# One transfer for a unit's q and k, one for its v, and most of the first bias loads on GpSimd's DMA queue

## The chip, the core and the metric

The kernel runs on one core of a Trainium2 chip. The metric is the device time of one execution in microseconds (us), here the median of three runs. One further execution was recorded by the hardware profiler; "the profile" and "the trace" are of that one. TensorE (PE) multiplies, VectorE (DVE) and ScalarE (ACT) do elementwise work, GpSimd (POOL) does some of it too, and SyncE (SP) issues DMA transfers.

## What is computed

Attention with a relative position bias, and a feed-forward layer behind it, cut to what matters:

```python
# q, k, v: (4, 8, 576, 64) f32;  w1 (1, 32), b1 (32), w2 (32, 8)
scores = q @ k.T / sqrt(64)
rel = log1p(abs(i - j)) / log1p(max(i, 1))           # 576 x 576
bias = relu(rel[..., None] @ w1 + b1) @ w2           # 576 x 576 x 8 heads
attn = softmax(scores + bias)                        # over the last axis
x = (attn @ v)   # 4 x 576 tokens by 8 heads x 64
out = leaky_relu(x @ w_in, 0.01) @ w_out             # (2304, 512) -> 2048 -> 512
```

The bias depends on the head and the two positions, not on the batch.

## The kernel before

The work has three stages. **Bias generation** makes the bias for all heads. Its 36 row groups of 16 rows each (the list `GEN`) go through four relu tiles (`gen_r`, on ACT at L120 and on DVE at L122, shared out by a plan that balances the two engines), matmuls (`gen_mm`, L133), two ACT copies out of PSUM (`gen_ev`, L140 and L141) and one write of 295.5 KB to DRAM (L152). These DRAM buffers are five chunks, "0", "1", "2", "3" of 128 rows and "M" of 64. **Attention** runs over 16 units; a unit is a pair of heads and one batch entry, and has nine tiles in the order A0, B0, A1, B1, M, A2, B2, A3, B3. A tile's scores are made on PE (L242, or L233 for M, in unit 0; L248 after that), DVE adds the bias and takes the extreme (L271), ACT takes the exponential (L279), PE transposes (L313, L317, L331), ACT copies out (L329), and a multiplication by v follows twice per unit (L350). **The feed-forward layer** comes last; its weights are converted during attention.

All row groups are issued before the first tile: `gen_tick(g)` is called for g = -1 to 38, and a tick makes the relu tiles of group g + 1, the matmuls of group g and the copies and the write of group g - 1. The bias tiles of the first pair of heads are read back from DRAM by `load_bias(0, c)`, called at given ticks: chunk 0 at tick 16, chunk 1 at 24, M at 27, chunks 2 and 3 at 37. Chunk 0 is complete with the write of tick 10, chunk 1 with that of tick 18, M with tick 20, chunk 2 with tick 28, chunk 3 with tick 36. A load of a numbered chunk is three transfers (L174 for the A tile, L175 and L176 for the B tile); M is two (L170, L171).

Every engine works through its own instructions in order, in the order of the calls in the source (a hand-written schedule). Every transfer but one is issued by SP, so a transfer that waits for data holds back the later ones. `load_unit` loads a unit's q and k with four transfers (L186): q into rows 0 to 63 and again into rows 64 to 127, then k in the same way. `load_v` loads v with one transfer (L192) and the last 64 keys with two small ones (L194) into a tile whose other half DVE sets to zero at the start (L68, L69). Units 0 and 1 are loaded before the bias generation, unit u + 2 during unit u.

GpSimd has hardly anything to do before 51 us: it makes an identity matrix, scales `w2` (L93), and then waits for the first subtraction of unit 1 (L213). It issues no transfer.

The lines that order all this at the start and at each tick:

```python
        gen_setup()
        for u in range(2):
            load_unit(u)
            load_v(u)
...
        for c in {16: "0", 24: "1", 27: "M", 37: "23"}.get(g, ()):
            load_bias(0, c)
```

Of the kernel before, what the change touches and what calls it, by code (L numbers as in the profile page):

```python
# [8 lines left out]
F32 = mybir.dt.float32  # L9
# [14 lines left out]
KW = 2 * S + 64  # L24
# [15 lines left out]


@with_exitstack
def attention_ffn(ctx: ExitStack, tc: tile.TileContext, qt, kt, vm, vt, wi, wo, cst, out):
    nc = tc.nc
    PS = bass.MemoryType.PSUM
    xp = ctx.enter_context(tc.tile_pool(name="xp", bufs=1))
# [12 lines left out]
    def pstile(tag):  # L59
        shape = [128, 1024] if tag == "s" else [128, 512]  # L60
        return ps.tile(shape, F32, tag=tag, name="ps_" + tag)

    raw_b = [[ap.tile([128, c], F32, name=f"raw{c}{i}") for c in (2 * S, KW)] for i in range(2)]
    ident = ap.tile([128, 128], F32, name="ident")
    make_identity(nc, ident[:])
    vt_b = [ap.tile([128, 2, 64], F32, name=f"vt{i}") for i in range(3)]
    for t in vt_b:
        nc.vector.memset(t[0:64, 1, :], 0.0)  # L68
        nc.vector.memset(t[64:128, 0, :], 0.0)  # L69
    qs_b = [ap.tile([128, 1024], F32R, name=f"qs{i}") for i in range(2)]  # L70

    PT = ap.tile([128, 2, 10, HS], F32, name="PT")

    raw_0 = [gp.tile([128, c], F32, name=f"raw{c}") for c in (2 * S, KW)]
    cs = gp.tile([128, S + 214], F32, name="cs")
    bps = gp.tile([128, 144], F32, name="bps")
    warm = gp.tile([128, 1], F32, name="warm")
# [23 lines left out]
    for T in GEN:  # L101
# [3 lines left out]
        eng = ""  # L105
# [6 lines left out]
    def gen_r(g):  # L112
        T = GEN[g]
        w = gen_w(T)
        r = gr[T] = [None] * 4
        for q, c in enumerate(plan[g]):
            k = 4 * T + q
            t = gp.tile([128, S], F32, tag="r", name="r", bufs=9)
            if c == "a":
                nc.scalar.activation(out=t[:, :w], in_=ltw[:, :w], func=AF.Relu, bias=bps[:, k:k + 1])  # L120
            else:
                nc.vector.tensor_scalar(out=t[:, :w], in0=ltw[:, :w], scalar1=bps[:, k:k + 1], scalar2=0.0, op0=ALU.add, op1=ALU.max)  # L122
            r[q] = t

    def gen_mm(T):
        r = gr.pop(T)
        w = gen_w(T)
        pt = pstile("s" if w > 512 else "to"[T % 2])
        cuts = [(0, w)] if w <= 512 else [(0, w // 2), (w // 2, w)]
        o0 = 512 - w // 2 if w > 512 else 0  # L130
        for a, b in cuts:
            for q in range(4):
                nc.tensor.matmul(pt[32 * q:32 * q + 32, o0 + a:o0 + b], w2d, r[q][:, a:b], start=True, stop=True)  # L133
        gps[T] = pt, o0

    def gen_ev(T):
        pt, o0 = gps.pop(T)
        R, F = 16 * T + 15, S - 16 * T
        e = e_b[GEN.index(T) % len(e_b)]
        nc.scalar.activation(out=e[:, R:W], in_=pt[:, o0:o0 + F], func=AF.Copy, scale=ips[:, T:T + 1])  # L140
        nc.scalar.activation(out=e[:, 0:R], in_=pt[:, o0 + R:o0:-1], func=AF.Copy, scale=ips[:, T:T + 1])  # L141
        if T < 16:
            c, r0 = str(T // 8), 16 * (T % 8)
        elif T < 18:
            c, r0 = "M", 16 * (T - 16)
        elif T < 34:
            c, r0 = str(2 + (T - 18) // 8), 16 * ((T - 18) % 8)
        else:
            c, r0 = "M", 32 + 16 * (T - 34)
        a = r0 * H * PIT + 1  # L150
        dst = scr[c][a:a + 16 * (H * PIT + 1)].rearrange("(i x) -> i x", i=16)[:, 0:H * PIT].rearrange("i (h p) -> i h p", h=H)[:, :, 0:W]
        nc.sync.dma_start(out=dst, in_=e)  # L152

    def gen_tick(g):
        if g + 1 < 36:
            gen_r(g + 1)
        if 0 <= g < 36:
            gen_mm(GEN[g])
        if 0 <= g - 1 < 36:
            gen_ev(GEN[g - 1])  # L160
        for c in {16: "0", 24: "1", 27: "M", 37: "23"}.get(g, ()):
            load_bias(0, c)
    bias = {}

    def load_bias(hp, c):
        n = 64 if c == "M" else 128
        rows = scr[c][0:n * H * PIT].rearrange("(i h p) -> i h p", h=H, p=PIT)[:, :, 16:16 + S]
        if c == "M":
            t = ap.tile([128, S], F32, tag="biasM", name="biasM", bufs=1)
            nc.sync.dma_start(out=t[0:64, :], in_=rows[:, 2 * hp, :])  # L170
            nc.sync.dma_start(out=t[64:128, :], in_=rows[:, 2 * hp + 1, :])  # L171
        else:
            t = ap.tile([128, 2, S], F32, tag="bias", name="bias", bufs=5)
            nc.sync.dma_start(out=t[:, 0, :], in_=rows[:, 2 * hp, :])  # L174
            nc.sync.dma_start(out=t[:, 1, 64:S], in_=rows[:, 2 * hp + 1, 0:512])  # L175
            nc.sync.dma_start(out=t[:, 1, 0:64], in_=rows[:, 2 * hp + 1, 512:S])  # L176
        bias[hp, c] = t

    raw, qk, vv = {}, {}, {}

    def load_unit(u):
        hp, b = divmod(u, B)
        q_, k_ = raw_b[u % 2] if u else raw_0
        for t, src in ((q_, qt), (k_, kt)):
            for p in (0, 64):
                nc.sync.dma_start(out=t[p:p + 64], in_=src[hp, b])  # L186
        raw[u] = (q_, k_)

    def load_v(u):
        hp, b = divmod(u, B)  # L190
        v_ = ap.tile([128, 4, 128], F32, tag="v", name="v", bufs=3)
        nc.sync.dma_start(out=v_[:], in_=vm[hp, b])  # L192
        for h in range(2):
            nc.sync.dma_start(out=vt_b[u % 3][64 * h:64 * h + 64, h, :], in_=vt[hp, b, h])  # L194
        vv[u] = v_

    def split_hi(u, what):
        q_, k_ = raw[u]
        if what == "q":
            qs = qs_b[u % 2]  # L200
            nc.vector.tensor_copy(qs[:].rearrange("p (a c) -> p a c", a=2), q_[:].rearrange("p (a c) -> p a c", a=2)[:, :, 64:S])  # L201
            ks1 = ap.tile([128, KW], F32R, tag="ks1", name="ks1", bufs=2)
            ks2 = ap.tile([128, KW], F32R, tag="ks2", name="ks2", bufs=2)
            qk[u] = (qs, ks1, ks2)
        else:
            nc.vector.tensor_copy(qk[u][1][:], k_[:])

    def split_lo(u, what, a):
        q_, k_ = raw[u]
# [128 lines left out]
    def pv():  # L338
        _, u, g = pv_q.pop(0)
        hp, b = divmod(u, B)  # L340
        o, pt = outs.pop((u, g)), PT[:, g]
        if (u, g) == (HP * B - 1, 1):
            o = pstile("s")
        for jb in range(5):
            for h in range(2):
                if jb < 4:
                    l, r = vv[u][:, jb, 64 * h:64 * h + 64], pt[:, 2 * jb + h, :]
                else:
                    l, r = vt_b[u % 3][:, h, :], pt[:, 8, :]
# [233 lines left out]
    with tc.manual_schedule():  # L583
# [249 lines left out]
```

## Time and profile before

| what | value |
|---|---|
| median of three runs | 684.1 us (684.05 to 684.8) |
| the profiled execution's own time | 684.88 us |
| its span, first to last instruction | 683.1 us |
| PE busy | 672.4 us, 98% of the span |
| DVE, ACT, POOL busy | 72%, 60%, 30% |
| moved by DMA | 117.85 MB, of them 116.96 on SP's queue |

The page of the profile cuts the span into 40 slices and gives the busy share of each engine in tenths. Timelines name a start, a duration, an engine, a line of the kernel, output and input tiles, a count where alike instructions stand together, and in brackets the time in which the engine stood idle before it and what ended that wait. A matmul's end is modelled, so that "busy" on PE covers some latency. DMA share is the mean busy share of the 16 DMA engines, including the time in which a packet waits.

### The profile page before, as it was taken

The numbers are of one execution on the slowest core, as the hardware profiler recorded it, in microseconds if no ns is written. First come the engines' busy times: TensorE is split into PE (matmuls) and PEld (weight loads), VectorE is DVE, ScalarE is ACT, GpSimd is POOL, SyncE is SP. The second block draws the span as 40 slices with busy tenths as digits, with TensorE's granted clock in tenths as the row PEclk, the third lists the DMA queues.
The fourth block names the chain that finished last, engine by engine and source line by source line (L and its number), as shares of the span: only waits on it lengthen the run. The fifth ranks groups of instructions, "written<-read, shape, count | busy, mean of one in ns | idle before, by whom it ended". The sixth has DMA issues, their size and how long they took to land.

```text
span 683.1 us, 11880 instructions
## 1 busy us (share of the span) xinstructions
PE 672.4 (98%) x4240; PEld 548.9 (80%) x4240; DVE 490.4 (72%) x1080; ACT 409.2 (60%) x886; POOL 205.8 (30%) x227
## 2 busy tenths in 40 slices
PE   7999999999999999999999999999999999999997
PEld 3436778887778777787889898888989898988986
DVE  7987789999999998589999868534343754343342
ACT  7997778888878888685555455333333543333332
POOL 0005445666666653420000503111114512111110
PEclk9999999999999999999999999999999999999999
DMA  8997679668955976135367336533323345332202
GB/s 226 350 315 198 198 224 245 170 203 276 272 165 164 315 217 197 57 114 199 94 201 244 141 95 230 196 113 108 107 108 108 121 175 197 140 109 108 107 1 92
DMA packets 39931, 117.85 MB, mean 173 GB/s; under 512 B 9024, under 2 KB 13760, under 8 KB 37440
## 3 DMA queue, kind: packets, MB, share of 16 engines
q1 hardware_dynamic: 39728, 116.96, 53.8%
q8 instruction: 33, 0.54, 0.3%
q14 instruction: 26, 0.21, 0.1%
q10 hardware_dynamic: 144, 0.13, 0.1%
HBM read 86.78 MB, written 30.29 MB: 171 GB/s over the span
## 4 chain that ended last, share of the span: by engine, by line
PE 92%; ACT 3%; DMA 3%; DVE 2%; issue 1%; SPq 0%; DVEq 0%; ACTq 0%
PE ps_t L516 24%; PE ps_s L557 19%; PE ps_o L350 12%; PE ps_s L248 10%; PE ps_o L557 10%; PE ps_t L313 9%; PE ps_s L233 1%; PE ps_o L302 1%; PE ps_o L331 1%; DMA w1a<-w 1%; ACT x L140 1%; ACT r L120 1%; PE ps_s L133 1%; PE ps_t L133 1%; PE ps_o L133 1%
## 5 line engine op out<-in xcount | busy, mean ns | idle before, releaser
L528 DVE TENSOR_TENSOR c<-ps_t,c 128x384 f32<-128x384 f32 x164 | 88.8, 554 | 130.5 <-PE ps_t L516 129.4
L535 ACT ACTIVATE g<-c 128x384 fp32r<-128x384 f32 x96 | 50.4, 525 | 180.8 <-DVE c L528 156.7
L557 PE MATMUL ps_s<-ws,g 128*128 128x512 f32 x576 | 148.3, 393 | 0.0
L557 PEld LDWEIGHTS ps_s<-ws,g 128*128 128x128 f32 x576 | 106.7, 188 | 16.9
L271 DVE CUSTOM_DVE_ANT_0 p<-ps_s,bias 128x576 f32<-128x576 f32 x128 | 95.4, 752 | 21.7 <-PE ps_s L248 18.0
L279 ACT ACTIVATE p<-p,mx 128x576 f32<-128x576 f32 x128 | 99.8, 780 | 7.8 <-DVE mx L271 5.5
L516 PE MATMUL ps_t<-xo,w1c 128*128 128x384 f32 x504 | 99.8, 336 | 0.7 <-DVE c L528 0.6
L466 POOL TENSOR_TENSOR ws<-y,ws 128x512 fp32r<-128x512 f32 x32 | 42.7, 1334 | 184.2 <-PE ps_t L516 147.4
L329 ACT COPY PT<-ps_t 128x512 f32<-128x512 f32 x128 | 73.8, 577 | 39.9 <-PE ps_t L313 39.9
L516 PEld LDWEIGHTS ps_t<-xo,w1c 128*128 128x128 f32 x504 | 89.3, 188 | 8.7 <-DVE c L528 2.3
L248 PE MATMUL ps_s<-ks,qs 128*128 128x288 f32 x480 | 93.7, 317 | 0.0
L516 PE MATMUL ps_t<-xo,w1a 128*128 128x384 f32 x474 | 93.2, 335 | 0.0
L516 PEld LDWEIGHTS ps_t<-xo,w1a 128*128 128x128 f32 x474 | 84.4, 188 | 5.9
L248 PEld LDWEIGHTS ps_s<-ks,qs 128*128 128x128 f32 x480 | 67.6, 189 | 13.3 <-issue 4.8
L313 PE MATMUL ps_t<-ident,p 128*128 128x128 f32 x512 | 77.5, 274 | 0.0
L557 PE MATMUL ps_o<-ws,g 128*128 128x512 f32 x288 | 74.1, 393 | 0.0
L540 DVE TENSOR_TENSOR g<-gf,g 128x384 fp32r<-128x384 f32 x96 | 61.1, 636 | 14.5 <-ACT gf L536 14.4
L313 PEld LDWEIGHTS ps_t<-ident,p 128*128 128x128 f32 x512 | 61.0, 140 | 9.1 <-issue 8.2
L350 PE MATMUL ps_o<-PT,v 128*64 128x288 f32 x496 | 67.0, 412 | 0.0
L213 POOL TENSOR_TENSOR qs<-raw,qs 64x512 fp32r<-64x512 f32 x30 | 37.8, 1279 | 75.4 <-DVE qs L201 72.0
L557 PEld LDWEIGHTS ps_o<-ws,g 128*128 128x128 f32 x288 | 53.4, 188 | 8.5
L350 PEld LDWEIGHTS ps_o<-PT,v 128*64 128x64 f32 x496 | 32.9, 136 | 23.6 <-issue 2.9
(127 smaller groups left out, 908.9 us busy)
## 6 DMA issues: line engine op xcount, KB each, us to landing
w1a<-w SPq DMA_DIRECT2D x10, 1792.0 KB, 7.4
w1c<-w SPq DMA_DIRECT2D x9, 1792.0 KB, 7.4
raw<-kt SPq DMA_DIRECT2D x32, 304.0 KB, 5.9
raw<-qt SPq DMA_DIRECT2D x32, 288.0 KB, 4.4
w<-w1a SPq DMA_DIRECT2D x20, 448.0 KB, 5.6
raw<-wi SPq DMA_DIRECT2D x16, 512.0 KB, 3.9
raw<-wo SPq DMA_DIRECT2D x16, 512.0 KB, 4.6
scr<-x SPq DMA_DIRECT2D x21, 295.5 KB, 5.0
```

The source lines that it names most:

```text
L248: nc.tensor.matmul(s_[:, S0 + HS * hh:S0 + HS * hh + HS], qs[:, c0:c0 + 128], ks[:, k0 + HS * hh:k0 + HS * hh + HS], start=(j == 0), stop= ...
L271: nc.vector.tensor_tensor_reduce(out=p, in0=s_[:, S0:S0 + S], in1=bt, scale=-0.125, scalar=3.4e38, op0=ALU.add, op1=ALU.min, accum_out=i)
L279: nc.scalar.activation(out=p, in_=p, func=AF.Exp, bias=i, scale=-1.0, accum_out=sm)
L313: nc.tensor.transpose(t0[:, 128 * jb:128 * jb + 128], p[:, p0 + 128 * jb:p0 + 128 * jb + 128], ident[:])
L329: nc.scalar.copy(out=PT[:, g, 0:8, c].rearrange("p (j h) c -> p j h c", h=2)[:, :, h, :], in_=t0[:].rearrange("p (j c) -> p j c", j=4))
L350: nc.tensor.matmul(o[64 * h:64 * h + 64, 0:HS], l, r, start=(jb == 0), stop=(jb == 4))
L466: eng.tensor_sub(t[:, 1], y2[c % MF][:], t[:, 0].bitcast(F32))
L516: nc.tensor.matmul(o, w[:, a, PROD[j], c], x[:, b, k, :], start=(n == 0), stop=(n == 5))
L528: nc.vector.tensor_add(a if c == src else c_new(g, c), bank[g, j], a)
L535: nc.scalar.activation(out=t[:, 0], in_=h, func=AF.Prelu, alpha=0.01)
L540: nc.vector.tensor_sub(t[:, 1], gf.pop((g, c))[:], t[:, 0].bitcast(F32))
L557: nc.tensor.matmul(o, t[:, a, c], w[:, b], start=(m == 0 and n == 0), stop=(m == NG - 1 and n == 5))
```

## The change

A unit's q and k come as one transfer of 128 rows from an input that the host has laid out that way (both copies of q and k stand in DRAM; 9472 bytes per row). v and its last 64 keys, zeros included, come as one transfer of five 128-column blocks; the small tiles, their two transfers and their zeroing go. `load_bias(0, c)` for c other than "3" is issued from GpSimd, and is called at other ticks: chunk 0 at 12 (was 16), 1 at 20 (24), M at 23 (27), 2 at 30 (37); chunk 3 stays on SP at 37. Loads for the later pairs of heads stay on SP. The matmul with the last 64 keys (L350) takes its weights from the fifth block.

```diff
-    raw_b = [[ap.tile([128, c], F32, name=f"raw{c}{i}") for c in (2 * S, KW)] for i in range(2)]
+    raw_b = [ap.tile([128, 2 * S + KW], F32, name=f"raw{i}") for i in range(2)]
...
-    vt_b = [ap.tile([128, 2, 64], F32, name=f"vt{i}") for i in range(3)]
-    for t in vt_b:
-        nc.vector.memset(t[0:64, 1, :], 0.0)
-        nc.vector.memset(t[64:128, 0, :], 0.0)
...
-        for c in {16: "0", 24: "1", 27: "M", 37: "23"}.get(g, ()):
+        for c in {12: "0", 20: "1", 23: "M", 30: "2", 37: "3"}.get(g, ()):
             load_bias(0, c)
...
     def load_bias(hp, c):
+        eng = nc.sync if hp or c == "3" else nc.gpsimd
...
-            nc.sync.dma_start(out=t[:, 0, :], in_=rows[:, 2 * hp, :])
-            nc.sync.dma_start(out=t[:, 1, 64:S], in_=rows[:, 2 * hp + 1, 0:512])
-            nc.sync.dma_start(out=t[:, 1, 0:64], in_=rows[:, 2 * hp + 1, 512:S])
+            eng.dma_start(out=t[:, 0, :], in_=rows[:, 2 * hp, :])
+            eng.dma_start(out=t[:, 1, 64:S], in_=rows[:, 2 * hp + 1, 0:512])
+            eng.dma_start(out=t[:, 1, 0:64], in_=rows[:, 2 * hp + 1, 512:S])
...
     def load_unit(u):
         hp, b = divmod(u, B)
-        q_, k_ = raw_b[u % 2] if u else raw_0
-        for t, src in ((q_, qt), (k_, kt)):
-            for p in (0, 64):
-                nc.sync.dma_start(out=t[p:p + 64], in_=src[hp, b])
-        raw[u] = (q_, k_)
+        t = raw_b[u % 2] if u else raw_0
+        nc.sync.dma_start(out=t[:], in_=qk_in[hp, b])
+        raw[u] = (t[:, 0:2 * S], t[:, 2 * S:2 * S + KW])

     def load_v(u):
         hp, b = divmod(u, B)
-        v_ = ap.tile([128, 4, 128], F32, tag="v", name="v", bufs=3)
-        nc.sync.dma_start(out=v_[:], in_=vm[hp, b])
-        for h in range(2):
-            nc.sync.dma_start(out=vt_b[u % 3][64 * h:64 * h + 64, h, :], in_=vt[hp, b, h])
+        v_ = ap.tile([128, 5, 128], F32, tag="v", name="v", bufs=3)
+        nc.sync.dma_start(out=v_[:], in_=v_in[hp, b])
         vv[u] = v_
...
-                if jb < 4:
-                    l, r = vv[u][:, jb, 64 * h:64 * h + 64], pt[:, 2 * jb + h, :]
-                else:
-                    l, r = vt_b[u % 3][:, h, :], pt[:, 8, :]
+                l, r = vv[u][:, jb, 64 * h:64 * h + 64], pt[:, 2 * jb + h if jb < 4 else 8, :]
```

## Rows read from the trace of the kernel before

**Rows 1.** The page's 40 slices of the span, TensorE
```profile
PE   7999999999999999999999999999999999999997
```

**Rows 2.** Windows: span, busy us (count) by engine, PE clock, DMA share, GB/s
```profile
6.00:8.00 2.00, 2.00 (x21) 1.24 (x17) 1.92 (x5) 1.26 (x4) 0.00 (x0) 1.00 0.99 224
16.00:18.00 2.00, 2.00 (x18) 0.87 (x14) 2.00 (x6) 2.00 (x6) 0.00 (x0) 1.00 1.08 402
```

**Rows 3.** The same windows, around the end of bias generation and unit 0
```profile
56.00:58.00 2.00, 1.50 (x11) 0.94 (x11) 1.46 (x6) 1.50 (x4) 1.09 (x4) 1.00 0.94 280
58.00:60.00 2.00, 2.00 (x16) 1.45 (x15) 1.88 (x6) 2.00 (x6) 2.00 (x2) 1.00 1.01 278
```

**Rows 4.** Timeline of VectorE and TensorE around unit 0's sixth and eighth tiles
```profile
53.42 1.11 DVE L206 CAST ks<-raw 128x1216 fp32r<-128x1216 f32 x1
...
55.70 0.76 DVE L271 CUSTOM_DVE_ANT_0 p<-ps_s,bias 128x576 f32<-128x576 f32 x1 [1.17 <-DMA bias<-scr]
55.74 0.27 PE L331 MATMUL ps_o<-ident,p 128*128 128x128 f32 x1
...
56.52 0.76 PE L242 MATMUL ps_s<-raw,raw 64*128 64x288 f32 x4 [0.50 <-DVE mx L271]
...
58.07 0.76 DVE L271 CUSTOM_DVE_ANT_0 p<-ps_s,bias 128x576 f32<-128x576 f32 x1 [0.58 <-DMA bias<-scr]
```

**Rows 5.** The chain that ended last: start, us, what
```profile
51.49 4.08 DMA bias<-scr
```

**Rows 6.** Timeline of SP's transfers: start, us to issue, count
```profile
1.63 1.24 SPq L186 DMA_DIRECT2D raw<-qt  x2
...
11.88 1.23 SPq L152 DMA_DIRECT2D scrM<-e  x2
...
26.82 0.55 SPq L174 DMA_DIRECT2D bias<-scr  x1
...
42.61 8.82 SPq L152 DMA_DIRECT2D scr<-x  x9
...
55.05 0.32 SPq L174 DMA_DIRECT2D bias<-scr  x1
```

**Rows 7.** Bias tiles until 65 us: issue ns least/median/most, landing
```profile
L174 SPq DMA_DIRECT2D bias<-scr x4: 320/574/813, 26.8 to 55.0; - x4
...
DMA to landing us min/median/max: 2.8/4.1/5.1
```

**Rows 8.** Timeline of VectorE: the start, the relu tiles of the generation, tile A0
```profile
3.51 0.30 DVE L90 TENSOR_SCALAR bps<-cs 128x144 f32<-128x144 f32 x1 [1.69 <-DMA cs<-cst]
3.72 0.65 DVE L92 TENSOR_SCALAR cs<-cs 128x320 f32<-128x320 f32 x2
...
13.51 33.93 DVE L122 TENSOR_SCALAR r<-cs,bps 128x496 f32<-128x496 f32 x96 [0.18 <-PE ps_s L133]
49.17 0.76 DVE L271 CUSTOM_DVE_ANT_0 p<-ps_s,bias 128x576 f32<-128x576 f32 x1 [1.73 <-PE ps_s L242]
```

**Rows 9.** Timeline of GpSimd: beside the first DVE work, and its next instruction
```profile
3.56 0.60 POOL L93 TENSOR_SCALAR cs<-cs 128x32 f32<-128x32 f32 x1 [2.28 <-DMA cs<-cst]
51.36 2.51 POOL L213 TENSOR_TENSOR qs<-raw,qs 64x512 fp32r<-64x512 f32 x2 [47.20 <-DVE qs L201]
```

**Rows 10.** Groups by shape until 400 us: busy us, mean ns, idle before
```profile
L122 DVE TENSOR_SCALAR r<-cs,bps 128x560 f32<-128x560 f32 x6 | 2.7, 508 | 0.0
...
L122 DVE TENSOR_SCALAR r<-cs,bps 128x304 f32<-128x304 f32 x7 | 2.2, 376 | 0.0
...
L292 POOL COPY pM<-pM 128x64 f32<-128x64 f32 x16 | 3.8, 239 | 0.0
```

**Rows 11.** The tile raw until 80 us, k's cast: least/median/most ns
```profile
L206 DVE CAST ks<-raw x2: 791/950/1108, 53.4 to 68.4; 128x1216 fp32r<-128x1216 f32 x2
```

**Rows 12.** Timelines: SP loads unit 3's q, and later VectorE casts it
```profile
67.46 1.10 SPq L186 DMA_DIRECT2D raw<-qt  x2
...
80.79 0.68 DVE L201 CAST qs<-raw 128x1024 fp32r<-128x1024 f32 x1
```

More of the change, by code (lines that the diff above doesn't have):

```diff
@@ L42, in attention_ffn @@
 @with_exitstack
-def attention_ffn(ctx: ExitStack, tc: tile.TileContext, qt, kt, vm, vt, wi, wo, cst, out):
+def attention_ffn(ctx: ExitStack, tc: tile.TileContext, qk_in, v_in, wi, wo, cst, out):
     nc = tc.nc
@@ L61, in pstile @@
         return ps.tile(shape, F32, tag=tag, name="ps_" + tag)
-    raw_b = [[ap.tile([128, c], F32, name=f"raw{c}{i}") for c in (2 * S, KW)] for i in range(2)]
+    raw_b = [ap.tile([128, 2 * S + KW], F32, name=f"raw{i}") for i in range(2)]
     ident = ap.tile([128, 128], F32, name="ident")
     make_identity(nc, ident[:])
-    vt_b = [ap.tile([128, 2, 64], F32, name=f"vt{i}") for i in range(3)]
-    for t in vt_b:
-        nc.vector.memset(t[0:64, 1, :], 0.0)
-        nc.vector.memset(t[64:128, 0, :], 0.0)
     qs_b = [ap.tile([128, 1024], F32R, name=f"qs{i}") for i in range(2)]
     PT = ap.tile([128, 2, 10, HS], F32, name="PT")
-    raw_0 = [gp.tile([128, c], F32, name=f"raw{c}") for c in (2 * S, KW)]
+    raw_0 = gp.tile([128, 2 * S + KW], F32, name="raw")
     cs = gp.tile([128, S + 214], F32, name="cs")
@@ L169, in load_bias @@
             t = ap.tile([128, S], F32, tag="biasM", name="biasM", bufs=1)
-            nc.sync.dma_start(out=t[0:64, :], in_=rows[:, 2 * hp, :])
-            nc.sync.dma_start(out=t[64:128, :], in_=rows[:, 2 * hp + 1, :])
+            eng.dma_start(out=t[0:64, :], in_=rows[:, 2 * hp, :])
+            eng.dma_start(out=t[64:128, :], in_=rows[:, 2 * hp + 1, :])
         else:
             t = ap.tile([128, 2, S], F32, tag="bias", name="bias", bufs=5)
-            nc.sync.dma_start(out=t[:, 0, :], in_=rows[:, 2 * hp, :])
-            nc.sync.dma_start(out=t[:, 1, 64:S], in_=rows[:, 2 * hp + 1, 0:512])
-            nc.sync.dma_start(out=t[:, 1, 0:64], in_=rows[:, 2 * hp + 1, 512:S])
+            eng.dma_start(out=t[:, 0, :], in_=rows[:, 2 * hp, :])
+            eng.dma_start(out=t[:, 1, 64:S], in_=rows[:, 2 * hp + 1, 0:512])
+            eng.dma_start(out=t[:, 1, 0:64], in_=rows[:, 2 * hp + 1, 512:S])
         bias[hp, c] = t
@@ L205, in split_hi @@
         else:
-            nc.vector.tensor_copy(qk[u][1][:], k_[:])
+            nc.vector.tensor_copy(qk[u][1][:], k_)
     def split_lo(u, what, a):
@@ L804 @@
     kd = np.concatenate([kd[0::2], kd[1::2, :, :, 512:], kd[1::2]], -1)
+    qkd = np.concatenate([qd.reshape(HP, B, D, 2 * S), kd], -1)
+    qkd = np.concatenate([qkd, qkd], 2)
     vd = v.transpose(1, 0, 2, 3).reshape(HP, 2, B, S, D).transpose(0, 2, 3, 1, 4).reshape(HP, B, S, 2 * D)
     vm = vd[:, :, :512].reshape(HP, B, 4, 128, 128).transpose(0, 1, 3, 2, 4)
-    vt = vd[:, :, 512:].reshape(HP, B, 64, 2, D).transpose(0, 1, 3, 2, 4)
+    vt = np.zeros((HP, B, 128, 1, 128), np.float32)
+    vt[:, :, :64, 0, :D] = vd[:, :, 512:, :D]
+    vt[:, :, 64:, 0, D:] = vd[:, :, 512:, D:]
+    vm = np.concatenate([vm, vt], 3)
     wi = inputs["moe_w_in"].reshape(KC, 128, MF, 128).transpose(2, 1, 0, 3).reshape(DFF, DM)
@@ L821 @@
     cst = np.concatenate([wb, np.repeat(psi, HID, axis=0), ipsi, np.repeat(lt, 128, axis=0)], axis=1)
-    arrays = {"qt": qd, "kt": kd, "vm": vm, "vt": vt, "wi": wi, "wo": wo, "cst": cst}
+    arrays = {"qk_in": qkd, "v_in": vm, "wi": wi, "wo": wo, "cst": cst}
     arrays = {n: np.ascontiguousarray(a) for n, a in arrays.items()}
```

2 lines of the change are left out of this document (1 added, 1 removed).

## The prediction

> **What bounds the kernel now.** I read the page's slices first: TensorE is at 9 tenths in every slice but the first and the last [rows 1], so whatever happens after some 60 us counts only if it leaves TensorE waiting. The first slices are another matter. The windows show bias generation with DVE busy 1.92 to 2.00 of 2.00 us and ACT, once it has its first matmuls, 2.00, while GpSimd does nothing and the DMA share is about 1 [rows 2]. DVE's timeline has 96 relu tiles without a gap from 13.51 to 13.51 + 33.93 = 47.44 us, and the first attention tile, A0, on DVE at 49.17 [rows 8]. So generation is bound by DVE and ACT, and no transfer holds it.
>
> The next stretch, unit 0, is where transfers count. Tile A2 starts on DVE at 55.70 after 1.17 us of waiting for a bias load, A3 at 58.07 after 0.58 us for another [rows 4]. The chain that ended last runs through the first of these loads, 51.49 to 55.57 us [rows 5]. TensorE's scores of A3 then start 0.50 us late, for want of the buffer that A2 holds [rows 4], and that is all that TensorE stands idle in the window 56 to 58 [rows 3]. From 58 us on TensorE is full and carries any delay or gain of its start to the end. The loads are late because SP has nine writes to issue from 42.61 to 51.43 us and only then comes to chunk 2, at 51.49 [rows 5]; chunk 3's, at 55.05, waits for its own last write to land [rows 6].
>
> **The change, part by part.** The profiled execution took 684.88 us, 1.8 more than its span of 683.1 and 0.78 more than the median; I apply each difference to the median, 684.1.
>
> *Chunk 2 comes sooner.* SP issues 36 writes between 11.88 and 51.43 us [rows 6], which makes 39.55/36 = 1.10 us per tick. Chunk 2 moves from tick 37 to 30: 51.49 - 7 x 1.10 = 43.8 us [rows 5]. A2 could start when DVE's cast ends, 53.42 + 1.11 = 54.53 [rows 4]. That leaves 10.7 us, of which landing takes 2.8 to 5.1, median 4.1 [rows 7], so 6.6 us are left for GpSimd's wait for the chunk's last writes and for three issues. If SP's issue times held there, 0.32 to 0.81 us each [rows 7], that is ample. The 1.17 us then go, and the 0.50 us on TensorE with them. What is late next is TensorE itself: its work before A3's scores ends at 55.74 + 0.27 = 56.01 [rows 4], which is 0.51 us before they start now. So TensorE bounds the gain at 0.50 us, DVE's two waits bound it at 1.17 + 0.58 = 1.75. I take 0.6, near the lower, because TensorE runs last from there on.
>
> *Chunk 3* stays on SP. If its last write lands as late as now, A3 stays at 58.07. It ends 0.76 us later, at 58.8, and TensorE is full from 58 on with other tiles between [rows 3, 4], so most of the 0.5 us survives. SP loses eleven bias issues (median 0.57 us for the first of a chunk [rows 7]), so the last writes may go out up to half a us sooner, but chunk 2's loads now pass the DMA engines ahead of them. I put zero for the pair.
>
> *Chunks 0, 1 and M* move by four ticks each, 4.4 us; chunk 0 from 26.82 to about 22.4, wanted at 49.17 [rows 6, 8]. Nothing waits for them now. GpSimd's queue has nothing else before 51.36 [rows 9], so a waiting load there holds back no computation but only the later loads. Gain nothing; cover 26.8 us for the first.
>
> *Unit loads.* Four issues become one and three become one. At the start SP's first write comes at 11.88 us [rows 6]; with ten issues fewer, at 1.24/2 = 0.62 us each [rows 6], it could go up to 6 us sooner, and no sooner than its data. The old loads fill 64 rows each and move 224 GB/s at a DMA share of 0.99, while the writes of 128 rows move 402 [rows 2]. The 3.0 MB of units 0 and 1 (2 x 1472 KB) would take 7.5 instead of 13.4 us at these rates. That shortens the queue of early writes, but ACT and DVE do not wait for them, so it gives nothing on the path. Later units are loaded early: unit 3's q is issued at 67.46 and first read at 80.79, 13.3 us later [rows 12]. One transfer of both, at worst as slow as four, still fits. Unit 2's loads stand behind chunk 3's wait on SP, as now.
>
> *Zeroing.* Six DVE instructions go. DVE waits 1.69 us for the constants before 3.51 us [rows 8], and these cover them; without that cover they would be some 1 us. The wider v adds 32 KB to 288 per unit, hidden as before.
>
> *GpSimd issues transfers.* This is the unknown: the trace has none. Eleven are added: 3 + 3 + 2 + 3. DVE's relu tiles take 508 ns for 560 columns and 376 for 304, 0.52 ns per column [rows 10]. The nearest row of GpSimd beside such work is L93: 0.60 us for 32 columns from 3.56 us [rows 9], while a copy of twice as many takes 0.24 elsewhere [rows 10]. So GpSimd lost some 0.4 us, yet it came through among DVE instructions that followed each other without a gap, from 3.51 and 3.72 on, 0.65 us for the two at 3.72 [rows 8]. In the other direction, DVE's cast of k takes 791 to 1108 ns [rows 11]; the long one, at 53.42 [rows 4], began while GpSimd subtracted from 51.36 to 53.87 [rows 9], so DVE lost 0.32 us. Per transfer, then, DVE loses between nothing and 0.32 us; a cost below zero is excluded, since DVE has no wait in generation to give back. GpSimd's own time per transfer lies between SP's least, 0.32, and SP's most with two losses as at L93, 0.81 + 2 x 0.4 = 1.6 us; three of the latter, 4.8, still fit in the 6.6 of chunk 2. I take zero for DVE, as at L93, because that row lies among the same kind of DVE work, without gaps. Sum: -0.6, so **683.5**, with 682.9 to 684.2 as its own range (from A2's 1.17 us given back to none, within a tenth).
>
> **The rivals.**
>
> *DVE is held up.* If each of the eleven transfers costs DVE the 0.32 us of the cast, generation ends 3.5 us later, as DVE has no idle time there [rows 8]: 684.1 + 3.5 - 0.6 = **687.0**. It is slower by over 0.2% (1.37 us) from 0.18 us per transfer. For it: DVE is full. Against it: L93.
>
> *GpSimd is starved.* Relu tiles without gaps [rows 8] leave GpSimd no room to prepare transfers until 47.44. Then chunk 0's three, at 0.57 us each and 4.1 to landing, are there at 53.3 instead of at 49.85 for B0; the rest follow at 0.57 us and keep pace with the tiles. That is +3.4 - 0.6: **686.9**. It decides if chunk 0's transfers aren't prepared by about 45 us. Against it: L93, which came through between such instructions [rows 8, 9].
>
> The Trainium skill, "SBUF — State Buffer", section "SBUF: two separate sides", warns of just this: GpSimd writes the descriptors of the transfers that it issues, and DVE in a mode that uses two ports keeps it out for the length of an instruction. By that rule alone the result would be this rival's 686.9 rather than 683.5; no row here shows a transfer of GpSimd, and L93 is a computation.
>
> *The early transfers collide.* Chunk 2's 576 KB, at the 280 GB/s of the window 56 to 58 [rows 3], take 2.1 us of the DMA engines just ahead of chunk 3's last writes. If these land that much later, A3 starts at 60.2 instead of 58.07. The buffer that it holds is wanted by TensorE about one DVE tile (0.76 us [rows 4]) after it would have been free, so I let 1.5 us of the 2.1 reach TensorE: 684.1 + 1.5 - 0.6 = **685.0**. Against it: the unit loads give some 5.9 us of DMA time back before.
>
> *DVE leads, not TensorE.* Busy time on TensorE is partly latency, and if it can follow DVE, the whole 1.75 us comes back: **682.3**. Against it: it needs chunk 3 early as well.
>
> *The change doesn't do what it says*: the loads are no sooner, since GpSimd takes as long as SP's queue did. That is 684.1, inside the first range.
>
> **How the numbers follow.** About 0.2% (1.37 us) is what a measurement of this kernel can tell from no change. Chances: forecast 0.40; no sooner loads 0.02; collision 0.08; DVE held 0.23; GpSimd starved 0.15; DVE leads 0.12. So faster 0.12, same 0.50, slower 0.38. The range runs from 682.6 to 687.4: it takes in the forecast's own range and most of both slow cases, and leaves out half of the fast case and the worst of the slow ones.
>
> **What would show it.** Right: A2 starts without a wait for bias, at about 54.5; relu tiles keep 0.52 ns per column and end at 47.4; A0 stays at 49.2; TensorE has no idle time in 56 to 58. DVE held: relu tiles with gaps or longer ones at the ticks of the loads, A0 after 50.5. Starved: GpSimd's transfers land after 50 us, DVE waits for bias at A0. Collision: A3 waits longer than 0.58 us. A change in attention or the feed-forward layer beyond the shifted start would make my reading of the stages wrong.

## The result and the profile after

The changed kernel takes 690.51 us (median of four runs, 689.39 to 691.95) against 684.45 us for the kernel before in the same session (684.05 to 685.28). The ratio is 1.0089, with a 95% interval of 1.0077 to 1.0101: slower by 6.1 us, above the range that was predicted. The profiled execution took 690.44 us, its span is 688.3 (before: 684.88 and 683.1).

I read GpSimd first, because the prediction left its price open. This is its timeline in the changed kernel (start, us, engine, line, what; in brackets the idle time before and its end). L171 to L173 are a chunk's three loads, L206 is unit 1's subtraction, which was L213.

```profile
23.33 23.60 POOL L171 DMA_DIRECT2D bias<-scr  x1 [19.12 <-DMA scr<-x]
46.92 0.55 POOL L172 DMA_DIRECT2D bias<-scr  x1
...
50.08 0.53 POOL L168 DMA_DIRECT2D biasM<-scrM  x1
51.60 0.57 POOL L171 DMA_DIRECT2D bias<-scr  x1 [0.99 <-DMA bias<-scr]
...
54.84 2.50 POOL L206 TENSOR_TENSOR qs<-raw,qs 64x512 fp32r<-64x512 f32 x2 [0.67 <-DVE qs L194]
```

The first load of chunk 0 has its data at 23.33 us, and GpSimd then spends 23.60 us on it, until 46.93. The next seven take about 0.54 us each. So the eight transfers of chunks 0, 1 and M all go out in one burst, from 46.93 to 50.61 us.

What ended at that time stands in the timeline of VectorE of the changed kernel (L118 is the relu of [rows 8], L264 the bias addition that was L271):

```profile
6.12 40.67 DVE L118 TENSOR_SCALAR r<-cs,bps 128x576 f32<-128x576 f32 x112 [0.27 <-PE ps_t L129]
...
51.46 0.76 DVE L264 CUSTOM_DVE_ANT_0 p<-ps_s,bias 128x576 f32<-128x576 f32 x1 [4.66 <-DMA bias<-scr]
...
53.29 0.76 DVE L264 CUSTOM_DVE_ANT_0 p<-ps_s,bias 128x576 f32<-128x576 f32 x1 [1.06 <-DMA bias<-scr]
...
56.86 0.76 DVE L264 CUSTOM_DVE_ANT_0 p<-ps_s,bias 128x576 f32<-128x576 f32 x1 [1.07 <-DMA bias<-scr]
```

DVE ran 112 relu tiles without a gap until 6.12 + 40.67 = 46.79 us, and GpSimd's first load came out 0.14 us later. A0 now waits 4.66 us for its bias and starts at 51.46, not at 49.17 as in [rows 8]; B0 and B1 wait again.

TensorE in the same stretch, first its timeline in the changed kernel (L235 and L241 are the scores of unit 0 and of unit 1, which were L242 and L248), then tile B0 and unit 1's first scores in the kernel before, then the windows of the changed kernel (span; busy us and count of PE, PEld, DVE, ACT, POOL; granted clock, DMA share, GB/s):

```profile
52.28 1.33 PE L235 MATMUL ps_s<-raw 64*128 64x288 f32 x4 [3.35 <-DVE mx L264]
54.11 1.33 PE L235 MATMUL ps_s<-raw 64*128 64x288 f32 x4 [0.49 <-DVE mx L264]
...
64.40 0.78 PE L241 MATMUL ps_s<-ks,qs 128*128 128x288 f32 x4
```

```profile
49.85 0.75 DVE L271 CUSTOM_DVE_ANT_0 p<-ps_s,bias 128x576 f32<-128x576 f32 x1
```

```profile
59.46 0.77 PE L248 MATMUL ps_s<-ks,qs 128*128 128x288 f32 x4
```

```profile
48.00:50.00 2.00, 0.94 (x8) 0.39 (x4) 0.00 (x0) 0.71 (x2) 2.00 (x4) 1.00 0.85 150
50.00:52.00 2.00, 0.00 (x0) 0.00 (x0) 0.54 (x1) 0.00 (x0) 1.01 (x3) 1.00 0.87 277
...
54.00:56.00 2.00, 1.89 (x7) 1.14 (x8) 1.46 (x5) 1.05 (x3) 1.33 (x2) 0.50 1.04 397
```

TensorE stands idle for 3.35 us, and then its granted clock is 0.50, so 1.2 instead of 2.4 GHz, in the windows 54 to 56 and 56 to 58 (0.56 just before, 0.73 from 58 to 60, and 1.00 after that). Four score matmuls take 1.33 us at 54.11, 0.76 in [rows 4]. Unit 1's first scores come at 64.40 us, against 59.46 in the trace before: 4.94 us late, and nothing after that gives it back.

The chain that ended last (start, us, what) shows how the 4.94 us come about:

```profile
47.45 5.67 DMA bias<-scr
...
53.29 0.76 DVE p L264
...
54.11 1.33 PE ps_s L235 x4
```

It runs through chunk 0's third transfer to B0, which starts at 53.29 instead of 49.85, 3.44 us late. From 54.11 us to unit 1 it is TensorE alone: B0 to unit 1 takes 11.11 us instead of 9.61, and these 1.50 us fall into the stretch of the lower clock. The later waits for bias, of A1, B1 and M, lie beside this chain.

SP, from which GpSimd's queue was meant to take work, comes late too. Its timeline in the changed kernel, L148 a write of generation and L171 chunk 3's load:

```profile
38.69 10.57 SPq L148 DMA_DIRECT2D scr<-x  x10
58.12 0.35 SPq L171 DMA_DIRECT2D bias<-scr  x1
```

The last write is issued at 49.26 us, sooner than the 51.43 of before, but chunk 3's load starts at 58.12, not at 55.05 [rows 6]: it waits 8.2 us for the last writes, which land late beside the burst.

### The profile page after: what moved, and what is told of

It is laid out like the page before. It is cut to its first block, busy times and chain, and to the rows that moved or that the text cites. A ratio compares the mean times of both kernels' runs of the same rounds, so it can differ in the third digit from the quotient of the medians.

```text
span 688.3 us, 11709 instructions
## 1 busy us (share of the span) xinstructions
PE 674.2 (98%) x4240; PEld 550.0 (80%) x4240; DVE 490.0 (71%) x1074; ACT 409.5 (60%) x886; POOL 234.7 (34%) x238
## 4 chain that ended last, share of the span: by engine, by line
PE 89%; ACT 4%; DVE 3%; DMA 2%; issue 1%; POOL 0%; ACTq 0%; DVEq 0%
PE ps_t L506 24%; PE ps_s L547 19%; PE ps_o L340 12%; PE ps_s L241 10%; PE ps_t L306 10%; PE ps_o L547 10%; PE ps_s L226 2%; ACT r L116 1%; PE ps_o L324 1%; PE ps_o L295 1%; ACT x L136 1%; DMA bias<-scr 1%; ACT e L136 1%; DVE xo L495 1%; DVE c L518 1%
## 5 line engine op out<-in xcount | busy, mean ns | idle before, releaser
L264 DVE CUSTOM_DVE_ANT_0 p<-ps_s,bias 128x576 f32<-128x576 f32 x128 | 95.7, 752 | 27.0 <-PE ps_s L241 18.5
L241 PE MATMUL ps_s<-ks,qs 128*128 128x288 f32 x480 | 93.7, 317 | 0.0
L340 PE MATMUL ps_o<-PT,v 128*64 128x288 f32 x620 | 82.0, 411 | 0.0
L241 PEld LDWEIGHTS ps_s<-ks,qs 128*128 128x128 f32 x480 | 67.6, 189 | 13.3 <-issue 6.1
L340 PEld LDWEIGHTS ps_o<-PT,v 128*64 128x64 f32 x620 | 41.8, 136 | 29.7 <-issue 2.9
L526 ACT ACTIVATE gf<-c 128x384 f32<-128x384 f32 x96 | 48.9, 509 | 0.0
```

The costliest lines, as they stand in the source:

```text
L241: nc.tensor.matmul(s_[:, S0 + HS * hh:S0 + HS * hh + HS], qs[:, c0:c0 + 128], ks[:, k0 + HS * hh:k0 + HS * hh + HS], start=(j == 0), stop= ...
L264: nc.vector.tensor_tensor_reduce(out=p, in0=s_[:, S0:S0 + S], in1=bt, scale=-0.125, scalar=3.4e38, op0=ALU.add, op1=ALU.min, accum_out=i)
L526: nc.scalar.activation(out=gf[g, c][:], in_=h, func=AF.Prelu, alpha=0.01)
```

## The experiments

Theory: GpSimd can't make a transfer while DVE's relu instructions follow each other without a gap; chunks 0, 1 and M come late, and that is the loss. Rivals: the merged unit loads are to blame; GpSimd's transfers are slow in themselves or crowd the DMA engines; the new, earlier ticks cost something on any queue; the clock is the loss. Ratios are to runs of the kernel before on the same chip, with 95% intervals.

### The parts of the change, one at a time

**queue_only**: the old unit loads, with the new ticks and GpSimd's queue.

```diff
-        for c in {16: "0", 24: "1", 27: "M", 37: "23"}.get(g, ()):
+        for c in {12: "0", 20: "1", 23: "M", 30: "2", 37: "3"}.get(g, ()):
...
+        eng = nc.sync if hp or c == "3" else nc.gpsimd
```

> Loads of q, k and v as before (seven transfers a unit); only load_bias(0, c) changes: GpSimd's queue and the new ticks. Starved (GpSimd cannot prepare a transfer while DVE runs relu tiles without a gap): the first transfer's issue on GpSimd lasts until within 0.3 us of the end of the relu tiles (47 us), the rest take 0.54 us each, and the time is 689.5 to 691.5, as with the whole change. Merged loads to blame for a part: 686 to 688.5.

Measured: 690.85 us, ratio 1.0092 (1.0079 to 1.0105). The timeline of GpSimd:

```profile
26.74 20.13 POOL L175 DMA_DIRECT2D bias<-scr  x1 [22.59 <-DMA scr<-x]
```

With the old unit loads the load starts 3.4 us later than in the changed kernel and yet ends at the same moment, 46.87 us. Its 20.13 us are no duration of its own; they last until the relu row ends (46.74 here). The merged loads are not to blame.

**sp_old**: the merged unit loads alone; bias loads on SP at the old ticks.

```diff
-        for c in {12: "0", 20: "1", 23: "M", 30: "2", 37: "3"}.get(g, ()):
+        for c in {16: "0", 24: "1", 27: "M", 37: "23"}.get(g, ()):
...
-        eng = nc.sync if hp or c == "3" else nc.gpsimd
+        eng = nc.sync
```

> Merged loads alone: bias loads on SP at the old ticks. Both hold that generation is bound by DVE and ACT: 684.0 to 684.7, the first bias write on SP at 8 us instead of 11.9, A2 still waiting for bias by 0.5 to 1.2 us. Merged loads to blame: above 685.5.

Measured: 684.38 us, ratio 0.9997 (0.9989 to 1.0006): nothing, although SP's first write goes out at 7.95 us instead of 11.88. The timeline of VectorE still has both waits of [rows 4], at A2 and A3:

```profile
55.66 0.76 DVE L264 CUSTOM_DVE_ANT_0 p<-ps_s,bias 128x576 f32<-128x576 f32 x1 [1.14 <-DMA bias<-scr]
...
57.73 0.76 DVE L264 CUSTOM_DVE_ANT_0 p<-ps_s,bias 128x576 f32<-128x576 f32 x1 [0.28 <-DMA bias<-scr]
```

**sp_new**: the merged unit loads and the new ticks, with all bias loads on SP.

```diff
-        eng = nc.sync if hp or c == "3" else nc.gpsimd
+        eng = nc.sync
```

> The whole change, but all bias loads stay on SP's queue, at the new ticks. Starved: nothing is left to starve, A2 starts without a wait for bias at about 54, and the time is 683.6 to 684.4 (up to 0.8 below before). Merged loads to blame: above 685.5, with waits for q, k or v in the trace.

Measured: 686.69 us, ratio 1.0041 (1.0023 to 1.0059), a miss; I had expected a small gain or nothing. A2 no longer waits, but A3 does. The timeline of SP, then that of VectorE at A3:

```profile
40.16 4.16 SPq L148 DMA_DIRECT2D scr<-x  x4
45.87 0.33 SPq L171 DMA_DIRECT2D bias<-scr  x1
...
48.20 4.61 SPq L148 DMA_DIRECT2D scr<-x  x6
56.25 0.33 SPq L171 DMA_DIRECT2D bias<-scr  x1
```

```profile
59.12 0.76 DVE L264 CUSTOM_DVE_ANT_0 p<-ps_s,bias 128x576 f32<-128x576 f32 x1 [3.49 <-DMA bias<-scr]
```

Chunk 2's load stands at the head of SP's queue from 44.32 to 45.87 us, 1.4 us of that until its own data is in DRAM. The last six writes stand behind it and start at 48.20; chunk 3 is loaded at 56.25 instead of 55.05 [rows 6], and A3 starts at 59.12 instead of 58.07 [rows 4]. The trace is of an execution of 685.67 us, and the twelve executions differ in the clock: seven with a mean granted clock of 0.999 to 1.000 took 685.38 to 686.96 us, five with 0.995 to 0.997 took 688.11 to 690.57. The wait in this trace speaks for the seven only; of the five there is no trace.

**ticks_only**: the kernel before with nothing but the new ticks.

```diff
-        for c in {16: "0", 24: "1", 27: "M", 37: "23"}.get(g, ()):
+        for c in {12: "0", 20: "1", 23: "M", 30: "2", 37: "3"}.get(g, ()):
```

> The new ticks alone: loads of q, k and v as before, bias loads on SP. Starved: 683.6 to 684.6; A2's wait of 1.17 us shrinks or goes. If SP's queue then holds the writes back behind loads that wait for their chunk to land, generation's last writes come later and A3 waits for longer than 0.58 us: up to 685.5.

Measured: 691.21 us, ratio 1.0098 (1.0086 to 1.0110), a worse miss. The timeline of SP, then VectorE at A3 and TensorE at unit 1's first scores:

```profile
49.05 0.33 SPq L174 DMA_DIRECT2D bias<-scr  x1
...
51.08 5.05 SPq L152 DMA_DIRECT2D scr<-x  x6
59.77 0.33 SPq L174 DMA_DIRECT2D bias<-scr  x1
```

```profile
62.66 0.76 DVE L271 CUSTOM_DVE_ANT_0 p<-ps_s,bias 128x576 f32<-128x576 f32 x1 [6.75 <-DMA bias<-scr]
```

```profile
63.49 1.33 PE L248 MATMUL ps_s<-ks,qs 128*128 128x288 f32 x4 [5.00 <-DVE mx L271]
```

It is the same mechanism, larger: without the merged loads SP runs some 3 us later (chunk 2's load at 49.05 against 45.87 in sp_new), and A3 waits 6.75 us. TensorE stands idle for 5.00 us behind it, starts unit 1 4.0 us later than in the trace before, and runs these scores at the lower clock (1.33 us for 0.77). So the ticks are too early for any queue in which writes stand behind them. GpSimd's queue has no writes behind its loads, which is what the change is right about.

### What keeps GpSimd's transfers in

**pool_0o**: merged loads and old ticks, with chunk 0 alone on GpSimd at tick 12 and the rest on SP.

```diff
-        for c in {12: "0", 20: "1", 23: "M", 30: "2", 37: "3"}.get(g, ()):
+        for c in {12: "0", 24: "1", 27: "M", 37: "23"}.get(g, ()):
...
-        eng = nc.sync if hp or c == "3" else nc.gpsimd
+        eng = nc.gpsimd if not hp and c == "0" else nc.sync
```

> Merged loads, old ticks, and only chunk 0 through GpSimd at tick 12. If GpSimd's first transfer waits for the last relu tile whatever its tick, its three issues end at about 48.2, 24 us after the chunk is in DRAM. Landing of 4 us (no burst of eleven) puts A0 at about 51 and B0 at 52.5: 686.5 to 688.5. If the loss of the whole change came from the burst of eleven alone and not from the start, A0 stays at 49.2: 684 to 685.

Measured: 690.82 us, ratio 1.0091 (1.0078 to 1.0104), above what I had expected in either case. Three transfers through GpSimd cost as much as eleven. GpSimd's timeline, then VectorE's:

```profile
23.62 23.91 POOL L171 DMA_DIRECT2D bias<-scr  x1 [19.50 <-DMA scr<-x]
```

```profile
13.47 33.94 DVE L118 TENSOR_SCALAR r<-cs,bps 128x496 f32<-128x496 f32 x96 [0.18 <-PE ps_s L129]
...
52.72 0.76 DVE L264 CUSTOM_DVE_ANT_0 p<-ps_s,bias 128x576 f32<-128x576 f32 x1 [5.31 <-DMA bias<-scr]
```

Here the relu row ends 0.6 us later, at 47.41, and so does the load, at 47.53. A0 waits 5.31 us. The size of the burst is therefore not what decides: A0 needs chunk 0, and chunk 0's late loads are enough. A0 starts 3.55 us later than in [rows 8] (I had expected 51), B0 waits 0.72 us, and no tile after it waits for a bias before unit 1. Yet unit 1's scores come at 65.79, 6.33 us late: TensorE has a clock of 0.50 from 56 to 60 us, as in the changed kernel, and DVE waits for its scores.

**stt**: the changed kernel, with DVE's relu as an instruction of two inputs (the second is a tile of zeros).

```diff
-                nc.vector.tensor_scalar(out=t[:, :w], in0=ltw[:, :w], scalar1=bps[:, k:k + 1], scalar2=0.0, op0=ALU.add, op1=ALU.max)
+                nc.vector.scalar_tensor_tensor(out=t[:, :w], in0=ltw[:, :w], scalar=bps[:, k:k + 1], in1=zero[:, :w], op0=ALU.add, op1=ALU.max)
```

> The whole change, but DVE's relu tiles are made by an instruction with two tensor inputs (the second is a tile of zeros), which takes about twice as long per column. DVE is then even fuller, so generation gets longer by some 15 us. If any full DVE keeps GpSimd from preparing transfers, the first one still ends with the last relu tile (about 62 us). If it is the kind of instruction (0.52 ns per column), the first transfer takes about 0.55 us right when its chunk has landed, at about 25 us.

Measured in a single execution: 710.1 us, since DVE's relu is slower (0.59 us per tile, 68.71/117, against 0.36, 40.67/112). VectorE, then GpSimd:

```profile
4.35 68.71 DVE L120 SCALAR_TENSOR_TENSOR r<-cs,bps,zero 128x320 f32<-128x320 f32 x117
```

```profile
29.71 0.76 POOL L173 DMA_DIRECT2D bias<-scr  x1 [25.47 <-DMA scr<-x]
30.46 0.55 POOL L174 DMA_DIRECT2D bias<-scr  x1
...
61.97 0.57 POOL L173 DMA_DIRECT2D bias<-scr  x1 [8.69 <-DMA scr<-x]
```

DVE runs 117 of these without a gap from 4.35 to 73.06 us (the row ends 26 us later than in the changed kernel, not some 15), and every load goes out in 0.52 to 0.76 us as soon as its data has landed. So a full DVE is not the cause; this kind of DVE instruction is.

**window**: the changed kernel, with one DVE copy of a single column at tick 17 that reads ACT's output.

```diff
+        if g == 17:
+            nc.vector.tensor_copy(warm[:], e_b[(g - 1) % len(e_b)][:, 0:1])
```

> The whole change with one small DVE copy at tick 17 that waits for ACT, so that DVE stands idle for 1 to 3 us at about 25 us. If GpSimd only needs a gap in DVE's work, the first transfer ends within it, 20 us sooner than now, and one to five transfers get out; chunk 0 is then in time for A0 and the rest still waits for 47 us: 689 to 692, with the gap's own cost. If the first transfer has a long start of its own, it ends at about 47 as before.

Measured in a single execution: 690.32 us. GpSimd, then VectorE:

```profile
23.23 3.81 POOL L173 DMA_DIRECT2D bias<-scr  x1 [19.09 <-DMA scr<-x]
27.04 0.61 POOL L174 DMA_DIRECT2D bias<-scr  x1
...
35.03 12.08 POOL L173 DMA_DIRECT2D bias<-scr  x1 [6.85 <-DMA scrM<-e]
```

```profile
26.95 0.15 DVE L158 COPY warm<-x 128x1 f32<-128x1 f32 x1
27.02 19.97 DVE L118 TENSOR_SCALAR r<-cs,bps 128x576 f32<-128x576 f32 x56
...
48.69 0.76 DVE L266 CUSTOM_DVE_ANT_0 p<-ps_s,bias 128x576 f32<-128x576 f32 x1 [1.70 <-PE ps_s L237]
```

A break of under 0.2 us in the relu row lets chunk 0 out at 27.04; A0 starts at 48.69 without waiting for bias. But chunk 1's load, ready at 35.03, is held until 47.11, and tile A1 waits 2.48 us for it at 53.29. The total stays where it was, again with a clock of 0.50, from 56 to 62 us: chunk 0 alone (pool_0o) is enough for the loss, and so are the chunks behind it.

**gaps**: so, six such copies.

```diff
+        if g in (14, 18, 22, 26, 30, 34):
+            nc.vector.tensor_copy(warm[:], e_b[(g - 1) % len(e_b)][:, 0:1])
```

> The changed kernel with six DVE copies of one column, at row groups 14, 18, 22, 26, 30 and 34, each reading what ACT has just written, so that DVE is free for a moment six times. If GpSimd's transfers are late only because DVE's unbroken row of relu instructions keeps them in, chunk 0's transfers go out near 23.7 us, chunk 1's by 37 and M's behind them, not at 47; the first score tile is corrected at 48.4 to 49.5 without a wait for its bias, TensorE's clock stays at full level, and what is left is what chunk 2 costs by being early (the fourth A tile waits some 3.5 us, as with all first loads on SP's queue): 685.8 to 687.5 us. If GpSimd's queue is slow for a reason of its own, so that its transfers pile up or land late even when let out, some score tile still waits over 4 us and the time stays at 689 to 691 us. If the copies themselves disturb DVE's row by over 0.3 us each, the last relu instruction ends after 48.5 us and the time rises by as much.

Measured: 685.89 us, ratio 1.0012 (1.0001 to 1.0023). Of the 6.1 us, about 5 are gone (685.89 is 1.1 above the kernel before). GpSimd, then VectorE:

```profile
34.60 3.49 POOL L173 DMA_DIRECT2D bias<-scr  x1 [8.54 <-DMA scrM<-x]
38.09 0.67 POOL L174 DMA_DIRECT2D bias<-scr  x1
...
46.79 1.75 POOL L173 DMA_DIRECT2D bias<-scr  x1 [6.22 <-issue]
```

```profile
38.07 0.15 DVE L158 COPY warm<-e 128x1 f32<-128x1 f32 x1
...
50.12 0.76 DVE L266 CUSTOM_DVE_ANT_0 p<-ps_s,bias 128x576 f32<-128x576 f32 x1 [1.64 <-PE ps_s L237]
...
59.35 0.76 DVE L266 CUSTOM_DVE_ANT_0 p<-ps_s,bias 128x576 f32<-128x576 f32 x1 [1.98 <-DMA bias<-scr]
```

Chunk 1's load is held from 34.60 until the copy at 38.07 (I had expected 37), chunk 2's until the relu row ends at 48.42. A0 waits for TensorE and no longer for bias, though it starts 0.6 us later than I allowed, at 50.12, because with the copies the relu row ends at 48.42 and not at 46.79. The granted clock stays at 1.00 in every window from 46 to 64. What is left goes with A3's wait. This is the experiment that settles the main cause.

### What is left: chunk 2 before chunk 3's writes

**pool_2o**: merged loads and old ticks, with chunk 2 alone on GpSimd, at tick 30.

```diff
-        for c in {12: "0", 20: "1", 23: "M", 30: "2", 37: "3"}.get(g, ()):
+        for c in {16: "0", 24: "1", 27: "M", 30: "2", 37: "3"}.get(g, ()):
...
-        eng = nc.sync if hp or c == "3" else nc.gpsimd
+        eng = nc.gpsimd if not hp and c == "2" else nc.sync
```

> Merged loads, old ticks, and only chunk 2 through GpSimd at tick 30. If a GpSimd transfer is prepared only after the last relu tile, at 46.9 to 48.5, chunk 2 lands at 52 to 54.5, just in time for A2 at 54.5: 683.4 to 684.6. If its transfers crowd out chunk 3's last writes, A3 waits for over 1 us: 684.5 to 686.

Measured: 685.95 us, ratio 1.0022 (1.0011 to 1.0033). GpSimd, then VectorE at A3:

```profile
45.99 0.94 POOL L171 DMA_DIRECT2D bias<-scr  x1 [41.83 <-DMA scr<-x]
```

```profile
59.35 0.76 DVE L264 CUSTOM_DVE_ANT_0 p<-ps_s,bias 128x576 f32<-128x576 f32 x1 [3.60 <-DMA bias<-scr]
```

The relu row holds this load for under 1 us, and the load stands in nobody's way on SP. A2 starts at 53.79 without a wait. Yet A3 starts at 59.35, 1.28 us later than before [rows 4]: chunk 3's load goes out at 56.52 after 3.4 us of waiting for the last writes. These were issued by 50.50, sooner than the 50.72 of sp_old, where chunk 3's load went out at 54.51; so here it is their landing that is late, not their issue.

**sp_33**: merged loads, all on SP, with chunk 2 at tick 33 and the rest at the old ticks.

```diff
-        for c in {12: "0", 20: "1", 23: "M", 30: "2", 37: "3"}.get(g, ()):
+        for c in {16: "0", 24: "1", 27: "M", 33: "2", 37: "3"}.get(g, ()):
...
-        eng = nc.sync if hp or c == "3" else nc.gpsimd
+        eng = nc.sync
```

> Merged loads, all bias loads on SP, old ticks but chunk 2 at tick 33 instead of 37, when its writes have landed. If what hurt with the new ticks on SP is that a load waits at the head of the queue for its chunk to land, there is no such wait here: A2 starts without a wait, A3's load is late by at most 1.5 us: 683.6 to 684.8. If any earlier load delays chunk 3's writes, A3 waits over 2 us: 685 to 687.

Measured: 685.37 us, ratio 1.0013 (1.0004 to 1.0021). VectorE at A3:

```profile
58.77 0.76 DVE L264 CUSTOM_DVE_ANT_0 p<-ps_s,bias 128x576 f32<-128x576 f32 x1 [2.37 <-DMA bias<-scr]
```

Between the two settings the trade goes on: A2's wait is gone (54.42), A3's is larger, and the sum is a little worse than sp_old. Chunk 2's load goes out at 47.41 here, without a wait at the head of the queue, so what it costs chunk 3 is the place in the queue (the last write is issued by 52.55, in sp_old by 50.72) and perhaps on the DMA engines.

### The clock

**pe_busy**: the changed kernel, with TensorE transposes that nobody reads: 32 where it waits for the first bias, and six ahead of each of the next three score tiles.

```diff
+            if n in (1, 2, 3, 4):
+                d = pstile("t")
+                for x in range(32 if n == 1 else 6):
+                    nc.tensor.transpose(d[:, 128 * (x % 4):128 * (x % 4) + 128], ident[:], ident[:])
```

> The whole change with some 50 extra transposes of the identity on TensorE after the second to fifth tiles, whose results nobody reads. If the granted clock of 0.5 from 52.2 to 59.1 us costs time of its own, it stays at 1.0 here, the tiles' scores take 0.76 us instead of 1.33, and the time is 689 to 690. If DVE waits for bias anyway until M at 58, the time stays at 690 to 691.

Measured: 690.42 us, ratio 1.0085 (1.0072 to 1.0098), no gain although the clock stays at 1.00. The test was spoilt in part by its own means: each six transposes took 0.82 to 0.87 us on TensorE's path, and A0's bias came 1.6 us later than in the changed kernel's trace (53.03 against 51.46), for a reason that isn't shown.

**pe_warm**: so, the 32 alone.

```diff
+            if n == 1:
+                d = pstile("t")
+                for x in range(32):
+                    nc.tensor.transpose(d[:, 128 * (x % 4):128 * (x % 4) + 128], ident[:], ident[:])
```

> The changed kernel with 32 TensorE transposes whose result nobody reads, in the 3.5 us in which TensorE waits for the first bias, and nowhere else (an earlier kernel also had six of them ahead of each of the next three score tiles, 0.82 to 0.87 us each on TensorE's own path). If the fall of the granted clock to 0.50 carries part of the loss, the stretch from the first corrected score tile to unit 1's first scores falls from 12.9 us in the changed kernel towards the 11.1 us of the kernel before, and the time to 688.3 to 689.2 us. If the late biases carry it all, that stretch is as long as in the changed kernel, with the waits for bias grown by what TensorE gained, and the time stays at 690 to 691 us.

Measured: 690.06 us, ratio 1.0068 (1.0045 to 1.0092). The expectation gives 11.1 us for the kernel before from A0 to unit 1's first scores; the traces give 59.46 - 49.17 = 10.3. Windows and TensorE of pe_warm:

```profile
54.00:56.00 2.00, 1.41 (x12) 0.79 (x15) 1.73 (x5) 0.96 (x3) 1.22 (x2) 1.00 1.03 405
```

```profile
63.11 0.78 PE L241 MATMUL ps_s<-ks,qs 128*128 128x288 f32 x4
```

In the trace the clock counts: from A0 (51.91) to unit 1 (63.11) takes 11.2 us instead of the changed kernel's 12.9. From B0 (53.59) it takes 9.52 instead of 11.11, close to the 9.61 of the kernel before, although M waits for its bias here too (0.28 us); the span is 687.0 instead of 688.3. In pool_0o B0 (54.20) to unit 1 takes 11.59. So the traces put the clock at some 1.5 us in the changed kernel and 2.0 in pool_0o. The times don't confirm it: 690.06 and 690.51 can't be told apart, since the two intervals overlap. How much of the 6.1 us the clock carries therefore stays open. It is in any case a consequence of the idle TensorE, not a second cause: in gaps, where TensorE doesn't wait, the clock doesn't fall.

## Why the prediction was wrong

The forecast was 683.5 us, and 690.51 were measured.

**The step that failed** is the price of a transfer on GpSimd: "GpSimd's own time per transfer lies between SP's least, 0.32, and SP's most with two losses as at L93", 1.6 us. The upper bound came from L93, a computation of 0.60 us beside DVE work [rows 9]. It is no near row. L93 ran beside three DVE instructions that were over after 0.86 us, at 4.37 [rows 8]; the transfer was kept out by 67 relu tiles without a gap (those in the trace from 23.33 us to the end of the row). The first transfer took 23.60 us, nearly fifteen times my upper end. The price isn't one per transfer at all; it is the time until DVE's row has a break or ends (23.60, 20.13 and 23.91 us with a row that ends at 46.79, 46.74 and 47.41; 3.81 and 3.49 with a break at 26.95 and 38.07). Of the price to DVE, "I take zero for DVE" was right: the last 96 tiles take 33.94 us in pool_0o and 33.93 in [rows 8].

The Trainium skill, "SBUF — State Buffer", section "SBUF: two separate sides", says that GpSimd can't write descriptors while DVE runs an instruction that uses two ports, and its section "Who interferes with whom" names the one-input arithmetic of the relu tiles among those that can, and a two-input instruction as one that keeps out only GpSimd's reads. The traces agree on the two kinds: 23.60 us for the first load beside the one, 0.76 beside the other (stt). On the length they go further than the rule, which speaks of a single instruction: here the load was kept out for the whole row. I set that rule below a row that didn't bear on it.

**GpSimd is starved**, the rival with 0.15, was right in its mechanism, and in its place: B0 at 53.3 us worked out, 53.29 measured. That this agrees so closely is luck: chunk 0's transfers were through at 47.99 and not at 49.15, and the last of them landed after 5.7 us, not 4.1 [rows 7]. The rival's time was low, 686.9 against 690.5. One missing term is TensorE at half clock, with 1.33 us for 0.76: by the chain above it makes 1.50 of the 4.94 us, with B0's 3.44 (the sum has 3.4). The "-0.6" in that sum was also not there. With both, the sum would be 689.0; the spans of the two traces differ by 5.2 us and the medians by 6.1, and these 0.9 us aren't explained. That "the rest follow at 0.57 us and keep pace with the tiles" was wrong as well: the loads issued from 40 to 52 us landed after 6.7 to 7.7 us (medians by line), and A1, B1 and M waited 0.33, 1.07 and 0.38 us. But these waits lie beside the chain.

**Chunk 2 sooner gives 0.6 us** failed by itself, apart from GpSimd. Its first half is right: given an early chunk 2, A2 starts at 53.66 to 54.42 without a wait (sp_new, pool_2o, sp_33), near the 54.53 worked out. But "I put zero for the pair" of effects on chunk 3 was wrong: A3 then waits 2.37 to 3.60 us, and no such kernel is faster than before. That is the collision rival's mechanism, with 685.0 worked out and 685.37 to 685.95 measured for chunk 2 alone (sp_33, pool_2o); it had a chance of only 0.08. DMA engines with little room there (share 0.99 and 0.97 in the windows 46 to 48 and 48 to 50 of the trace before) would explain the late landing in pool_2o; in sp_33 the place in SP's queue does it too.

**SP's queue at the new ticks** was not in the prediction. I gave the tick of a load no price if its data is ready in time; but the ticks let loads reach the head of SP's queue before it was, and ticks_only lost 6.7 us by that and by the clock that fell in the wait.

**Unit loads and zeroing** were right: nothing on the path (sp_old, 0.9997), and the first write 3.9 us sooner, under the 6 allowed. Later units and the feed-forward layer don't move: unit 1 starts 4.94 us late and the span is 5.2 us longer. *DVE is held up* was wrong, as the relu row shows.

No kernel here beats the kernel before. All that was to be had was A2's 1.17 and A3's 0.58 us, of which TensorE itself waited for 0.50 [rows 4], and every setting that removed the first enlarged the second.

## What to carry to other kernels

Before a transfer is moved to GpSimd's queue, look at what DVE runs when it will be issued: here a row of one-input arithmetic without gaps held the first load to the end of the row, and the others landed together with it. A price for a new kind of work must come from a row of that kind, and where there is none the wide end is the length of the whole row, not that of a few instructions. And a load that is issued earlier takes its place from something: ask which write or load now stands behind it, and who waits for that.

## What was not expected of the hardware

- A single break of under 0.2 us let GpSimd in, and what followed directly then passed too: in gaps the held transfer came out at 38.09, just after the copy at 38.07, and four more followed by 40.57 us while DVE had its relu row again from 38.14. After 6.22 us of idling, GpSimd's next load was held again. Why the followers pass, and whether it is the pause or the copy itself that lets the first one in, was not tried.
- While GpSimd's transfers leave in a burst, SP's writes land late: of those issued from 36 to 52 us the median is 3.3 us to landing in the changed kernel but the slowest takes 9.3, against 4.6 and 5.6 in the kernel before, and all transfers together move 150 GB/s in the window 48 to 50, against 308. Which side holds up which is open.
- The clock fell to 0.50 after TensorE had stood idle for 2.59 us (window), 3.35 (the changed kernel), 3.99 (pool_0o), 4.80 (queue_only) and 5.00 (ticks_only). It stayed at 1.00 after 1.74 (sp_new) and 1.84 us (pool_2o), and where the idle time was 1.36 us behind 32 transposes (pe_busy).
